# Clustered attention and two MLPs on one core: a pool per weight buffer, two products ahead of each second layer, the last MLP 1 pair by batch

## The chip, the core and the metric

The kernel runs on one core of a Trainium2 chip. The metric is the device time of one execution in microseconds (us). Five engines work beside each other: TensorE (PE in the profile; its weight loads stand as PEld), VectorE (DVE), ScalarE (ACT), GpSimd (POOL) and SyncE (SP), which issues the DMAs. Each takes its own instructions in order and waits on semaphores for the others.

## What is computed

Three blocks follow each other. Two batches, eight heads, 768 positions, head size 64; the two MLPs have 1536 tokens, a model width of 512, and inner widths of 2048 and 1536.

```python
mask = argmax(q_n . c_n) == argmax(k_n . c_n)           # same cluster of 16
attn = softmax(where(mask, scale * q @ k.T, -1e9)) @ v
x = attn, heads side by side                            # (1536, 512)
h = x @ w_in;   x = (h * sigmoid(h)) @ w_out            # MLP 1
out = (sigmoid(x @ w_gate) * (x @ w_val)) @ w_out2      # MLP 2
```

The weights come as 64-bit floats. All matmuls have operands split into a high and a low half, and three products (high x high, high x low, low x high) make one.

## The kernel before

**Order.** The kernel is written against a planner that places each engine's instructions: they have the priority of the order in which the code issues them, and the planner takes what it reckons to be ready. A tile pool gets a stretch of memory; pools that are closed give theirs to pools opened later, which then wait for the work on what lay there. Tiles of one tag in a pool share its buffers.

**Attention** (L101 to L529) runs over eight pairs of heads, four per batch. `raw` and `st` hold a pair's loaded and split queries and keys until `prep` (L328) has prepared it, `hd` (L105, one pool per parity of the pair) its heads and values, `cp` tables, among them `q2` and `k2` of both parities (L207), and `wk` what goes from step to step. `finish` (L457) scales a pair's result into `acc` (L54), which holds the activations between the blocks. For batch 0, the operands of MLP 1 are made on POOL during the second half of attention (L476 to L481).

**Operands.** `right_operands` (L73) makes seven operands per batch from the four blocks of `acc` in the manner of Strassen: 11, 21, t2, t1, t3, t4, 22, with four additions, seven casts to a high half (ACT) and seven subtractions for the low half (DVE or POOL). It yields eight times.

**MLP 1** takes the inner width in eight pairs of 128-column blocks (`N1`, L540). `hidden` (L686) computes a pair by `strassen` (L637): seven products x, y, x again, z, v, w, w again, each of twelve matmuls for both batches or six for one. `take` applies SiLU, and `split` (L677) writes the high half (ACT) and the low half (POOL or DVE) into the four buffers of `gp`. `mixed` (L700) is the second layer: it multiplies them into `acc`, in four or six tiles that `accumulate` (L694) adds, on DVE, or copies for pair 0, on ACT. Pair 0 runs batch by batch; so does the second layer of the last pair, and the operands of MLP 2 are made after each batch of it (`operands`, L727, y).

**MLP 2** has six pairs (`N2`). `gated` (L747) runs `strassen` twice, for the gate and for the value, `out_of` (L766) is its second layer, in six tiles of twelve matmuls.

**Weights.** A job (L601) makes one weight: `converted` (L542) loads 512 KB into one of two buffers `rp` and builds 32-bit words from it on ACT, POOL and DVE; `two` (L558) splits into high and low halves, in seven buffers of `sp`, used in turn. `seven` (L570), for a first layer, takes three of them and one of two small ones (tag d); `plain`, for a second layer, takes one; so an MLP 1 pair takes 5, an MLP 2 pair 8. `weights` (L621) starts the jobs up to two ahead of the one asked for.

**Banks.** `pp` (L538) has four buffers of two PSUM banks, for products and second layers alike. The buffer of x is held from the first to the second half of x, that of w likewise.

These are the lines that the change moves against each other (L790):

```python
    for i in range(N2):
        for bs in (slice(0, 1), slice(1, 2)) if i == 0 else (ALL,):
            gated(i, bs)
        out_of(i)
```

Of the kernel before, what the change touches and what calls it, by code (L numbers as in the profile page):

```python
# [10 lines left out]
F32 = mybir.dt.float32  # L11
# [20 lines left out]
def clustered_attention_then_two_mlps(ctx, tc, qT, kT, v, cen, w1i, w1o, w2g, w2v, w2o, out):  # L32
# [40 lines left out]
    def right_operands(pool, temporary, name, b, caster, adder, subbers):  # L73
# [25 lines left out]
        yield  # L99

    with ExitStack() as att:  # L101
        raw = att.enter_context(tc.tile_pool(name="raw", bufs=1))
        st = att.enter_context(tc.tile_pool(name="st", bufs=1))

        hd = {p % 2: att.enter_context(tc.tile_pool(name=f"hd{p}", bufs=1)) for p in (NPAIR, NPAIR + 1)}  # L105
        cp = att.enter_context(tc.tile_pool(name="cp", bufs=1))
        wk = att.enter_context(tc.tile_pool(name="wk", bufs=2))
        sm = att.enter_context(tc.tile_pool(name="sm", bufs=4))
# [67 lines left out]

        wt = cp.tile([P, 512], BF16, tag="wt", name="wt")
        nc.vector.memset(wt, 0.0)
# [27 lines left out]

        q2, k2 = ([cp.tile([P, 2, S], R32, tag=f"{nm}_{i}", name=f"{nm}_{i}") for i in range(2)] for nm in ("q2", "k2"))  # L207

# [119 lines left out]
        def prep(p):  # L328
# [56 lines left out]
            for i in range(NT):  # L385
                nc.tensor.transpose(pt[:, i * P : (i + 1) * P], o[:, i].rearrange("p j n c -> p (j n c)"), identb)
            rows = wk.tile([P, S], F32, tag="rb", name=f"rows{p}")
            nc.scalar.activation(rows, pt[:, 0:S], AF.Identity, bias=rowbias, scale=rowscale)
# [9 lines left out]
        def scores(p, j, i):  # L398
            qa, qm, ka, km, _ = heads[p]
            s = ps_s.tile([P, 2, 512], F32, tag="s", name=f"s{p}_{j}_{i}")  # L400
            for n, (a, c) in enumerate(((qa, ka), (qm, km))):
                for g in range(2):
                    nc.tensor.matmul(  # L403
                        s[:, g, 0:HS],
                        lhsT=a[:, j, i * P : (i + 1) * P],
                        rhs=c[:, j, g * HS : (g + 1) * HS],
                        start=n == 0,
                        stop=n == 1,
                    )
            nm = sm.tile([P, 1], F32, tag="nm", name=f"nm{p}_{j}_{i}")  # L410
            nc.vector.tensor_reduce(nm, s[:, :, 0:HS], axis=AX.XY, op=ALU.max, negate=True)  # L411
            e = wk.tile([P, 2, HS], F32, tag="e", name=f"e{p}_{j}_{i}", bufs=4)
            if p not in tots:
                tots[p] = wk.tile([P, 2 * NT], F32, tag="tot", name=f"tot{p}")
# [23 lines left out]
        def values(p, j, g):  # L438
# [14 lines left out]
            if p not in xf:  # L453
                xf[p] = wk.tile([P, S], F32, tag="xf", name=f"xf{p}")
            nc.vector.tensor_tensor(xf[p][main, g * G : (g + 1) * G], o[main], other[main], op=ALU.add)  # L455

        def finish(p):  # L457
# [3 lines left out]
            nc.vector.tensor_scalar_add(t, t, 1e-9)  # L461
            rs = wk.tile([P, 2 * NT], F32, tag="rs", name=f"rs{p}")
# [3 lines left out]
            rt = wk.tile([P, P], F32, tag="rt", name=f"rt{p}")  # L466
            nc.scalar.activation(rt[0 : 2 * NT], pr[0 : 2 * NT, 0:P], AF.Copy)
            yield
            rb = wk.tile([P, S], F32, tag="rb", name=f"rb{p}")
            dma_rows(rb, rt)  # L470
# [86 lines left out]

    def two(src, name, tag="w", bufs=None):  # L558

        n = src.shape[1]  # L560
# [9 lines left out]
    def seven(srcs, name):  # L570
# [12 lines left out]
        s34 = two(t[:, 2:4].rearrange("p a b -> p (a b)"), f"{name}t")  # L583
        last = two(a22, f"{name}d", tag="d", bufs=2)

# [51 lines left out]
    def strassen(w, name, take, bs):  # L637
# [19 lines left out]
        u2 = temporary(f"{name}u")[:, bs]  # L657
        nc.scalar.activation(u2, x, AF.Copy)
        add(u2, run(bank(f"{name}y"), "s2", "t2"), u2)
        run(xb, "a12", "21", start=False)  # L660
        take(x, 0, 0, bs, False)
        u3 = temporary(f"{name}v")[:, bs]
        add(u3, run(bank(f"{name}z"), "s3", "t3"), u2)
        c21 = temporary(f"{name}c")[:, bs]
        nc.vector.tensor_tensor(c21, u3, run(bank(f"{name}v"), "a22", "t4"), op=ALU.subtract)
        take(c21, 1, 0, bs, True)
        qb = bank(f"{name}w")
        q = run(qb, "s1", "t1")
        add(u3, q, u3)
        take(u3, 1, 1, bs, True)  # L670
        run(qb, "s4", "22", start=False)
        add(u2, q, u2)
        take(u2, 0, 1, bs, True)

    gs = {}
# [10 lines left out]
    def hidden(i, bs):  # L686
# [4 lines left out]

        strassen(weights("1i", i), f"h{i}", take, bs)

# [6 lines left out]
    def mixed(i, b=None):  # L700
# [9 lines left out]
        for n, c in enumerate(parts):  # L710
            for e in range(2):
# [3 lines left out]
                for d in range(2):  # L715
                    for k, (fh, fl) in enumerate(f):
                        for m, (s, t) in enumerate(((wh, fh), (wh, fl), (wl, fh))):
# [6 lines left out]
                            )  # L724
                accumulate(z[:, 2 * e : 2 * e + 2, c], o[:, :, 0:width], i == 0)

    def operands(pool, name, b):  # L727
        for _ in right_operands(pool, temporary, name, b, nc.scalar, nc.vector, [nc.vector, nc.gpsimd]):
            pass

    for i in range(N1):
        if i == 0:
            for b in range(B):
                if b:
                    operands(tp, "x", b)
                hidden(i, slice(b, b + 1))
                mixed(i, b)
            continue
        hidden(i, ALL)
        if i < N1 - 1:  # L740
            mixed(i)
            continue
        for b in range(B):
            mixed(i, b)
            operands((xp, tp)[b], "y", b)

    def gated(i, bs):  # L747
# [11 lines left out]

        strassen(weights("2g", i), f"g{i}", gate, bs)  # L760
        strassen(weights("2v", i), f"v{i}", value, bs)

# [3 lines left out]
    def out_of(i):  # L766
        f = [[gs[f"b{i}", k, t].rearrange("p h b s -> p (h b s)") for t in "hl"] for k in range(2)]
        for t in range(0, B * S // P, 2):
# [14 lines left out]
            if i == N2 - 1:  # L783
                for a in range(2):
# [61 lines left out]
```

## Time and profile before

| | us |
|---|---|
| median of 3 runs (lowest to highest) | 885.61 (883.98 to 886.31) |
| the profiled execution | 891.42 |
| its span, first to last instruction | 889.6 |
| PE busy in it | 810.3 (91%) |
| DVE busy | 656.0 (74%) |
| POOL busy | 462.4 (52%) |
| ACT busy | 396.1 (45%) |

All durations below are of the profiled execution. A timeline row has the start, the time, the engine, the line, the operation, the tile written and the tiles read, with the shape; brackets hold the idle time of that engine before it and who ended it. Tile names have lost their numbers: `ghb` and `glb` are the high and low halves of a pair's activations in MLP 2 (`gha`, `gla` in MLP 1), `z` a second-layer tile of MLP 2 (`y` in MLP 1), `wh` and `wl` halves of a weight; `x11h` to `xt4l` are operands of MLP 1, `y11h` to `yt4l` of MLP 2.

### The profile page before, as it was taken

How to read it: one execution, taken by the hardware profiler on the slowest of the kernel's cores; microseconds unless marked ns; L12 is line 12 of the kernel's file. 1: busy time of each engine (PE TensorE's matmuls, PEld its weight loads, DVE VectorE, ACT ScalarE, POOL GpSimd, SP SyncE). 2: the span in 40 equal slices, each digit the busy share in tenths (PEclk: the TensorE clock that was granted, in tenths of full speed). 3: DMA queues.
4: the chain of work that ended last, by engine and by line, in shares of the span. 5: the costliest groups of instructions: out<-in, count | busy, mean ns of one | idle time of the engine just before them, and what ended most of it. 6: DMA issues, size and time to landing. Idle time of an engine off the chain costs nothing.

```text
span 889.6 us, 12086 instructions
## 1 busy us (share of the span) xinstructions
PE 810.3 (91%) x4539; PEld 699.0 (79%) x4539; DVE 656.0 (74%) x822; ACT 396.1 (45%) x679; POOL 462.4 (52%) x390
## 2 busy tenths in 40 slices
PE   6899999999996788999999999399969989898997
PEld 4777777777774687988988898398958969697896
DVE  5778877987986877687677668957784776757635
ACT  3556556556666554424524434444521514234020
POOL 4512260582307776547546557758682745747221
PEclk9999999999999799999999999689998989799899
DMA  7564465356310222121121120002221211111003
GB/s 214 142 156 110 115 165 132 100 143 153 122 43 19 95 95 90 53 95 48 48 95 48 48 95 24 25 24 93 73 70 50 72 47 67 53 48 48 1 1 142
DMA packets 25226, 72.50 MB, mean 81 GB/s; under 512 B 4144, under 2 KB 4240, under 8 KB 25168
## 3 DMA queue, kind: packets, MB, share of 16 engines
q1 hardware_dynamic: 25168, 71.73, 27.1%
q8 instruction: 36, 0.59, 0.3%
q14 instruction: 22, 0.18, 0.1%
HBM read 48.27 MB, written 3.19 MB: 58 GB/s over the span
## 4 chain that ended last, share of the span: by engine, by line
PE 66%; DVE 22%; ACT 4%; issue 4%; POOL 3%; DMA 1%; SPq 0%; DVEq 0%; ACTq 0%; POOLq 0%
PE z L774 10%; PE s L403 7%; PE v L443 6%; PE t L435 4%; PE h_0x L643 3%; PE g_0w L643 3%; PE v_0x L643 3%; DVE nm L411 3%; PE pm L140 2%; PE v_0w L643 2%; PE g_0x L643 2%; DVE gla L684 2%; PE u L430 2%; PE y_10None L718 2%; PE y_21None L718 2%
## 5 line engine op out<-in xcount | busy, mean ns | idle before, releaser
L416 ACT ACTIVATE e<-s,nm 128x768 f32<-128x768 f32 x96 | 86.5, 902 | 67.4 <-DVE nm L411 66.4
L411 DVE TENSOR_REDUCE nm<-s 128x1 f32<-128x768 f32 x96 | 90.9, 950 | 10.8 <-PE s L403 8.3
L443 PE MATMUL v<-ph,vv 128*64 128x256 f32 x576 | 75.5, 389 | 1.4 <-DVE xf L455 1.2
L774 PE MATMUL z<-whu,ghb 128*128 128x512 f32 x144 | 61.2, 425 | 14.0 <-ACT ghb L59 10.2
L403 PE MATMUL s<-ka,qa 128*128 128x384 f32 x192 | 59.5, 391 | 6.5 <-ACT e L416 6.4
L774 PE MATMUL z<-whu,glb 128*128 128x512 f32 x144 | 58.4, 434 | 4.7 <-DVE glb L684 4.7
L774 PE MATMUL z<-wlu,ghb 128*128 128x512 f32 x144 | 60.6, 421 | 0.0
L435 PE MATMUL t<-ident,e 128*128 128x128 f32 x384 | 57.9, 280 | 1.2 <-DVE ph L62 1.0
L443 PEld LDWEIGHTS v<-ph,vv 128*64 128x64 f32 x576 | 37.4, 137 | 24.9 <-issue 6.7
L698 DVE TENSOR_TENSOR acc<-z,acc 128x1024 f32<-128x1024 f32 x30 | 36.6, 1223 | 24.2 <-PE z L774 24.1
L403 PE MATMUL s<-k,q 128*128 128x384 f32 x192 | 51.6, 350 | 1.0 <-DVE k L320 1.0
L435 PEld LDWEIGHTS t<-ident,e 128*128 128x128 f32 x384 | 45.2, 143 | 6.9 <-issue 1.9
L341 POOL TENSOR_SCALAR qq<-qq 128x768 f32<-128x768 f32 x7 | 5.8, 834 | 82.5 <-DMA qq<-in_qT 70.3
L774 PEld LDWEIGHTS z<-whu,ghb 128*128 128x128 f32 x144 | 29.7, 206 | 22.7 <-ACT ghb L59 12.3
L403 PEld LDWEIGHTS s<-ka,qa 128*128 128x128 f32 x192 | 29.9, 195 | 20.4 <-ACT e L416 11.7
L474 POOL TENSOR_TENSOR acc<-xf,rb 128x768 f32<-128x768 f32 x7 | 12.8, 1832 | 58.8 <-DMA rb<-d_rb 52.5
L774 PEld LDWEIGHTS z<-whu,glb 128*128 128x128 f32 x144 | 30.1, 209 | 15.8 <-DVE glb L684 9.5
L59 ACT ACTIVATE ph<-t 128x512 f32<-128x512 f32 x48 | 28.6, 596 | 21.1 <-PE t L435 20.8
L430 PE MATMUL u<-ident,e 128*128 128x128 f32 x192 | 36.8, 280 | 0.2 <-DVE ph L62 0.2
L455 DVE TENSOR_TENSOR xf<-v,other 64x256 f32<-64x256 f32 x48 | 20.1, 419 | 22.3 <-ACT other L452 22.0
L403 PEld LDWEIGHTS s<-k,q 128*128 128x128 f32 x192 | 35.4, 194 | 1.5 <-DVE k L320 1.5
L62 DVE COPY ph<-t 128x512 f32<-128x512 f32 x48 | 32.7, 680 | 4.7 <-PE t L435 4.6
(1441 smaller groups left out, 2561.0 us busy)
## 6 DMA issues: line engine op xcount, KB each, us to landing
ri<-in_w1i SPq DMA_DIRECT2D x16, 512.0 KB, 3.2
ro<-in_w1o SPq DMA_DIRECT2D x16, 512.0 KB, 3.2
ka<-kh SPq DMA_DIRECT2D x32, 192.0 KB, 3.7
rg<-in_w2g SPq DMA_DIRECT2D x12, 512.0 KB, 3.2
rv<-in_w2v SPq DMA_DIRECT2D x12, 512.0 KB, 3.3
ru<-in_w2o SPq DMA_DIRECT2D x12, 512.0 KB, 3.1
qq<-in_qT SPq DMA_DIRECT2D x8, 384.0 KB, 4.8
kk<-in_kT SPq DMA_DIRECT2D x8, 384.0 KB, 4.6
```

The lines of the kernel that those rows point to most:

```text
L59: return nc.scalar.activation(o, i, AF.Copy)
L62: return nc.vector.tensor_copy(o, i)
L403: nc.tensor.matmul(s[:, g, 0:HS], lhsT=a[:, j, i * P : (i + 1) * P], rhs=c[:, j, g * HS : (g + 1) * HS], start=n == 0, stop=n == 1,)
L411: nc.vector.tensor_reduce(nm, s[:, :, 0:HS], axis=AX.XY, op=ALU.max, negate=True)
L416: nc.scalar.activation(e, s[:, :, 0:HS], AF.Exp, bias=nm, scale=1.0, accum_out=tots[p][:, n : n + 1])
L430: nc.tensor.transpose(both[:, kt - 4, i % GT, :], e[:, kt * P : (kt + 1) * P], ident)
L435: nc.tensor.transpose(t[:, kt, :], e[:, kt * P : (kt + 1) * P], ident)
L443: nc.tensor.matmul(o[(L, U)[kt % 2]], lhsT=vv[:, j, kt, :], rhs=ph[:, kt, :], start=kt < 2, stop=kt >= NT - 2,)
L643: nc.tensor.matmul(o[:, b, 0:HS], lhsT=w[a][s][:, k, :], rhs=right[b, q][t][:, k, :], start=start and k == 0 and n == 0, stop=k == KQ - 1 ...
L698: nc.vector.tensor_tensor(z, o, z, op=ALU.add)
L718: nc.tensor.matmul(o[:, d, 0:width], lhsT=s[:, d, k, :], rhs=t[:, c], start=k == 0 and m == 0, stop=k == 1 and m == 2,)
L774: nc.tensor.matmul(o[:, a, :], lhsT=s[:, (t + a) * P : (t + a + 1) * P], rhs=r, start=k == 0 and n == 0, stop=k == 1 and n == 2,)
```

## The change

- `rp` is opened ahead of attention and shares no memory with it. `q2` and `k2` get pools of their own (`qk`), each beside the `hd` pool of its parity. The tiles that a pair's end needs (`tot`, `xf`, `rs`, `rt`, `rb`) move from `wk` to a pool `fin` at the end.
- `sp` becomes seven pools of one buffer, each with a high and a low half, used in turn: five behind `wp` and the small pair's `dp`, two behind `up` and `gp`.
- `strassen` and `mixed` yield after each product and each tile, so that the loop over stages (pair, or pair and batch) can lay two generators side by side.
- Of each stage but a few, the first two products are issued ahead of the second layer of the stage before (`FRONT`): not for batch 1 of MLP 1's pair 0, and not for batch 1 of MLP 2's pair 0, whose batch 0 has no second layer of its own.
- The operands of MLP 1 for batch 1 are issued beside the products of batch 0 instead of after its second layer.
- The last pair of MLP 1 runs batch by batch altogether; the operands of MLP 2 are issued beside its second layers and the products of the stage after.

```diff
+    rp = ctx.enter_context(tc.tile_pool(name="rp", bufs=2))
     with ExitStack() as att:
...
-        hd = {p % 2: att.enter_context(tc.tile_pool(name=f"hd{p}", bufs=1)) for p in (NPAIR, NPAIR + 1)}
+        hd, qk = {}, {}
+        for p in (NPAIR % 2, (NPAIR + 1) % 2):
+            hd[p] = att.enter_context(tc.tile_pool(name=f"hd{p}", bufs=1))
+            qk[p] = att.enter_context(tc.tile_pool(name=f"qk{p}", bufs=1))
+        wk = att.enter_context(tc.tile_pool(name="wk", bufs=2))
         cp = att.enter_context(tc.tile_pool(name="cp", bufs=1))
-        wk = att.enter_context(tc.tile_pool(name="wk", bufs=2))
+        fin = att.enter_context(tc.tile_pool(name="fin", bufs=2))
...
-    rp = ctx.enter_context(tc.tile_pool(name="rp", bufs=2))
     wp = ctx.enter_context(tc.tile_pool(name="wp", bufs=3))
-    sp = ctx.enter_context(tc.tile_pool(name="sp", bufs=7))
+    dp = ctx.enter_context(tc.tile_pool(name="dp", bufs=2))
+    NSP = 7
+    sp = [ctx.enter_context(tc.tile_pool(name=f"sp{n}", bufs=1)) for n in range(NSP - 2)]
     up = ctx.enter_context(tc.tile_pool(name="up", bufs=8))
     gp = ctx.enter_context(tc.tile_pool(name="gp", bufs=1))
+    sp += [ctx.enter_context(tc.tile_pool(name=f"sp{n}", bufs=1)) for n in range(NSP - 2, NSP)]
+    taken = iter(range(10000))
...
-        hi = sp.tile([P, n], R32, tag=f"{tag}h", name=f"{tag}h{name}", bufs=bufs)
-        lo = sp.tile([P, n], R32, tag=f"{tag}l", name=f"{tag}l{name}", bufs=bufs)
+        w = (pool or sp[next(taken) % NSP]).tile([P, 2, src.shape[1]], R32, tag="w", name=f"w{name}")
+        hi, lo = w[:, 0], w[:, 1]
...
+    stages = []
+    for i in range(N1):
+        for b in range(B) if i in (0, N1 - 1) else (None,):
+            stages.append(("1", i, b))
     for i in range(N2):
-        for bs in (slice(0, 1), slice(1, 2)) if i == 0 else (ALL,):
-            gated(i, bs)
-        out_of(i)
+        for b in range(B) if i == 0 else (None,):
+            stages.append(("2", i, b))
+
+    def front(kind, i, b):
+        return (hidden if kind == "1" else gated)(i, ALL if b is None else ONE[b])
+
+    beside = operands(tp, "x", 1)
+    gen = front(*stages[0])
+    for n, (kind, i, b) in enumerate(stages):
+        steps(gen, beside)
+        following = stages[n + 1] if n + 1 < len(stages) else None
+        if following is not None:
+            gen = front(*following)
+        late = kind == "1" and i == 0 and b == 0
+        if following is not None and not late and not (kind == "2" and b == 0):
+            steps(gen, n=FRONT)
+        if kind == "1":
+            if i < N1 - 1:
+                steps(mixed(i, b), beside)
+                run(beside)
+            else:
+                run(beside)
+                beside = operands((xp, tp)[b], "y", b)
+                parts = mixed(i, b)
+                for c in range(4):
+                    next(parts)
+                    if c in (1, 2):
+                        next(beside)
+                run(parts)
+        elif b != 0:
+            run(beside)
+            out_of(i)
```

`steps` runs one generator and lays a step of another behind each of its steps, `run` runs one to its end, `FRONT` is 2, and `ONE[b]` selects one batch.

## Rows read from the trace of the kernel before

**Rows 1.** Windows by stage: PE, PEld, DVE, ACT, POOL us; clock; DMA; GB/s.

```profile
270.50:359.00 88.50, 71.20 (x338) 63.01 (x338) 69.87 (x73) 48.46 (x79) 66.59 (x56) 0.90 0.22 76
359.00:521.00 162.00, 156.18 (x782) 139.97 (x781) 115.50 (x127) 65.62 (x96) 92.25 (x80) 1.00 0.19 65
521.00:621.70 100.70, 83.81 (x422) 78.56 (x421) 77.81 (x83) 45.65 (x71) 69.56 (x54) 0.90 0.13 44
621.70:884.60 262.90, 243.91 (x1200) 219.68 (x1199) 174.98 (x172) 81.18 (x119) 138.21 (x119) 0.94 0.16 55
```

**Rows 2.** Chain of waits: start, us, engine, tile, line, count; starts of pairs.

```profile
359.05 2.10 PE h_0x L643 x12
521.16 2.10 PE h_0x L643 x12
621.70 2.10 PE g_0x L643 x12
679.11 2.10 PE g_0x L643 x12
838.97 2.10 PE g_0x L643 x12
870.22 14.34 PE z L774 x63
```

**Rows 3.** PE at MLP 2's boundaries: chain row, timeline (in brackets: idle before).

```profile
761.58 2.12 PE v_0w L643 x12
...
665.88 0.79 PE L774 MATMUL z<-whu,ghb 128*128 128x512 f32 x1 [2.97 <-DVE acc L698]
...
767.79 0.79 PE L774 MATMUL z<-whu,ghb 128*128 128x512 f32 x1 [2.72 <-ACT ghb L59]
771.39 0.80 PE L774 MATMUL z<-whu,glb 128*128 128x512 f32 x1 [0.85 <-DVE glb L684]
```

**Rows 4.** Windows: the stretch behind one boundary, columns as in rows 1.

```profile
770.00:780.00 10.00, 9.15 (x27) 6.83 (x26) 7.85 (x8) 0.00 (x0) 3.22 (x3) 0.62 0.14 52
```

**Rows 5.** Timeline there: POOL's weight half, DVE's split and accumulation.

```profile
751.92 1.30 POOL L564 TENSOR_TENSOR wlg4s<-sg,whg4s 128x512 fp32r<-128x512 f32 x1 [4.53 <-ACT whg4s L59]
...
768.76 2.57 DVE L684 TENSOR_TENSOR glb<-g_0v,ghb 128x768 fp32r<-128x768 f32 x1
783.67 1.23 DVE L698 TENSOR_TENSOR acc<-z,acc 128x1024 f32<-128x1024 f32 x1 [0.77 <-PE z L774]
```

**Rows 6.** Timeline at a boundary of MLP 1: POOL, PE.

```profile
457.13 1.29 POOL L564 TENSOR_TENSOR wli6s<-si,whi6s 128x512 fp32r<-128x512 f32 x1
...
478.24 0.50 PE L718 MATMUL y_10None<-gla,who 128*128 128x512 f32 x1 [1.17 <-DVE gla L684]
```

**Rows 7.** Timeline of the passage out of attention: ACT, POOL, PE, DVE.

```profile
225.35 0.68 ACT L551 ACTIVATE ci<-ri 128x512 f32<-128x512 f32 x1
...
263.08 1.83 POOL L474 TENSOR_TENSOR acc<-xf,rb 128x768 f32<-128x768 f32 x1 [20.07 <-DMA rb<-d_rb]
...
270.95 0.63 ACT L59 ACTIVATE whi0a<-ci 128x512 fp32r<-128x512 f32 x1
...
284.51 0.44 PE L643 MATMUL h_0w<-x22h,whi0t 128*128 128x384 f32 x1 [3.26 <-DVE h_0v L669]
...
295.20 0.95 DVE L70 TENSOR_TENSOR xt4l<-xt,xt4h 128x768 fp32r<-128x768 f32 x1
...
295.65 0.69 PE L718 MATMUL y<-gha,who 128*128 128x384 f32 x1 [4.80 <-ACT who L59]
```

**Rows 8.** Timeline of the passage between the MLPs: POOL, DVE, PE.

```profile
561.20 2.51 POOL L70 TENSOR_TENSOR y21l<-acc,y21h 128x768 fp32r<-128x768 f32 x1
...
561.97 2.55 DVE L70 TENSOR_TENSOR yt2l<-yt,yt2h 128x768 fp32r<-128x768 f32 x1
...
564.58 0.69 PE L643 MATMUL g_0y<-yt2l,whg0s 128*128 128x384 f32 x1 [6.02 <-DVE yt2l L70]
...
577.49 0.95 DVE L70 TENSOR_TENSOR yt4l<-yt,yt4h 128x768 fp32r<-128x768 f32 x1
```

More of the change, by code (lines that the diff above doesn't have):

```diff
@@ L174, in clustered_attention_then_two_mlps @@
         dma(kk, kT[0, 0])
-        wt = cp.tile([P, 512], BF16, tag="wt", name="wt")
+        wt = fin.tile([P, S], F32, tag="rb", name="wt").bitcast(BF16)[:, 0:512]
         nc.vector.memset(wt, 0.0)
@@ L203, in clustered_attention_then_two_mlps @@
         nc.scalar.activation(identb, ident, AF.Copy)
-        q2, k2 = ([cp.tile([P, 2, S], R32, tag=f"{nm}_{i}", name=f"{nm}_{i}") for i in range(2)] for nm in ("q2", "k2"))
+        q2, k2 = ([qk[i].tile([P, 2, S], R32, tag=nm, name=f"{nm}_{i}") for i in range(2)] for nm in ("q2", "k2"))
         oh = [cp.tile([P, NT, 2, 2, 32], BF16, tag=f"oh_{i}", name=f"oh_{i}") for i in range(2)]
@@ L386, in prep @@
                 nc.tensor.transpose(pt[:, i * P : (i + 1) * P], o[:, i].rearrange("p j n c -> p (j n c)"), identb)
-            rows = wk.tile([P, S], F32, tag="rb", name=f"rows{p}")
+            rows = fin.tile([P, S], F32, tag="rb", name=f"rows{p}")
             nc.scalar.activation(rows, pt[:, 0:S], AF.Identity, bias=rowbias, scale=rowscale)
@@ L413, in scores @@
             if p not in tots:
-                tots[p] = wk.tile([P, 2 * NT], F32, tag="tot", name=f"tot{p}")
+                tots[p] = fin.tile([P, 2 * NT], F32, tag="tot", name=f"tot{p}")
             n = j * NT + i
@@ L453, in values @@
             if p not in xf:
-                xf[p] = wk.tile([P, S], F32, tag="xf", name=f"xf{p}")
+                xf[p] = fin.tile([P, S], F32, tag="xf", name=f"xf{p}")
             nc.vector.tensor_tensor(xf[p][main, g * G : (g + 1) * G], o[main], other[main], op=ALU.add)
@@ L461, in finish @@
             nc.vector.tensor_scalar_add(t, t, 1e-9)
-            rs = wk.tile([P, 2 * NT], F32, tag="rs", name=f"rs{p}")
+            rs = fin.tile([P, 2 * NT], F32, tag="rs", name=f"rs{p}")
             nc.vector.reciprocal(rs, t)
@@ L583, in seven @@
         s34 = two(t[:, 2:4].rearrange("p a b -> p (a b)"), f"{name}t")
-        last = two(a22, f"{name}d", tag="d", bufs=2)
+        last = two(a22, f"{name}d", dp)
         def part(pair, n):
@@ L666, in strassen @@
         take(c21, 1, 0, bs, True)
+        yield
         qb = bank(f"{name}w")
@@ L673, in strassen @@
         take(u2, 0, 1, bs, True)
+        yield
     gs = {}
@@ L690, in take @@
             split(g, m, h, bs, f"a{i}", nc.gpsimd if h == 0 else nc.vector)
-        strassen(weights("1i", i), f"h{i}", take, bs)
+        yield from strassen(weights("1i", i), f"h{i}", take, bs)
     def accumulate(z, o, first):
@@ L725, in mixed @@
                 accumulate(z[:, 2 * e : 2 * e + 2, c], o[:, :, 0:width], i == 0)
+                yield
     def operands(pool, name, b):
[L728 to L745, printed above, removed]
+        return right_operands(pool, temporary, name, b, nc.scalar, nc.vector, [nc.vector, nc.gpsimd])
     def gated(i, bs):
@@ L788, in out_of, with steps, run @@
                     nc.sync.dma_start(out[n : n + P, :], z[:, a])
-    for i in range(N2):
-        for bs in (slice(0, 1), slice(1, 2)) if i == 0 else (ALL,):
-            gated(i, bs)
-        out_of(i)
+    def steps(main, beside=iter(()), n=None):
+        for _ in main:
+            next(beside, None)
+            if n is not None:
+                n -= 1
+                if n == 0:
+                    return
+    def run(gen):
+        for _ in gen:
+            pass
+    ONE = [slice(b, b + 1) for b in range(B)]
+    FRONT = 2
+    stages = []
+    for i in range(N1):
+        for b in range(B) if i in (0, N1 - 1) else (None,):
+            stages.append(("1", i, b))
+    for i in range(N2):
+        for b in range(B) if i == 0 else (None,):
[28 more added lines that the diff above has]
+            out_of(i)
 def _layout(i):
```

16 lines of the change are left out of this document (10 added, 6 removed).

## Prediction

> **What bounds the kernel now.** I read the busy time by stage first [rows 1]. The two MLPs run from 270.5 to 884.6 us. TensorE (PE) is the fullest engine in each of their four stages: 71.2 of 88.5 us in the passage out of attention, 156.2 of 162.0 in the steady part of MLP 1, 83.8 of 100.7 in the passage between the MLPs, 243.9 of 262.9 in the rest of MLP 2. VectorE (DVE) comes next with 69.9, 115.5, 77.8 and 175.0. So the question is what PE needs and what it loses.
>
> The chain of waits gives the need [rows 2]. A product of twelve 384-column matmuls takes 2.10 us, so one batch's half takes 1.05. The last 63 matmuls of 512 columns take 14.34 us, 0.228 each, so the 72 of one pair's second layer take 16.4. An MLP 1 pair needs 7 x 2.10 + 16.4 = 31.1 us, an MLP 2 pair 14 x 2.10 + 16.4 = 45.8; the last pair of MLP 2, from 838.97 to 870.22 + 14.34, takes 45.6, so this price is reached where nothing stands in the way. By batch a second layer is 96 matmuls of 384 columns, 96 x 2.10/12 = 16.8.
>
> What is lost, by the starts in [rows 2]:
> - Passage 1, from the end of attention (about 271.0, [rows 7]) to 359.05: 88.1 us for pairs 0 (14.7 + 16.8) and 1 (31.1), 62.6. Lost 25.5.
> - MLP 1, 359.05 to 521.16: five pairs at 32.4 against 31.1. Lost 1.3 each, 6.6 in all.
> - Passage 2, 521.16 to 621.70: 100.5 us for the last pair of MLP 1 (14.7 + 16.8) and pair 0 of MLP 2 (29.4 + 16.4), 77.3. Lost 23.2.
> - MLP 2: 621.70 to 679.11 is 57.4, the three pairs up to 838.97 take 53.3 each, against 45.8. Lost 11.6 + 3 x 7.5 = 34.1.
>
> Together 89 us. The profiled execution is 891.4 us, 889.6 of it span; the median of the three timed runs is 885.6, so 5.8 come off at the end.
>
> **Products ahead of the second layer, MLP 2.** PE's rows at one boundary [rows 3]: pair 3's last product ends at 763.70, some second-layer matmuls follow, then PE waits 2.72 us for ScalarE (ACT) and 0.85 for DVE, 3.6 in all. The other 4 us of the 7.5 are clock: in 770 to 780, after the wait, the granted clock is 0.62 of 2.4 GHz, so three quarters of that stretch ran at the 1.2 GHz level [rows 4]. The change puts two products of the next pair, 4.2 us, where the wait is. They must be ready then: the low half of the second weight they need is done at 753.2, ten us early [rows 5]. So 4.2 covers 3.6, and with PE kept busy I take the clock's fall to go too. MLP 1 supports that: its boundary wait of 1.17 us [rows 6] leaves the stage's clock at 1.00 [rows 1].
>
> What is late next is a bank. Four double banks serve products and second layer. The put-ahead product x holds one until its second half runs behind the second layer, y one until DVE has added it, so the second layer has two or three. One wait of this sort is there already: 2.97 us for the accumulation on DVE [rows 3]. An accumulation takes 1.23 us against 12 x 0.228 = 2.7 of PE work per bank [rows 5], which two banks bear unless DVE is held up; a split beside GpSimd (POOL) takes 2.57 [rows 5]. So I leave 2 to 2.5 us at each of four boundaries and take 25 of 34.1. Bounds: everything, 34; or the waits alone while the clock still falls, 4 x 3.6 = 14.
>
> The Trainium skill (Perfetto Trace Analysis, Matmul Optimizations and Identifying Performance Opportunities) wants all eight PSUM banks in use and reads a gap that repeats as a possible lack of buffers; it speaks against holding a bank. The 2.97 us above agree with it once; what it would do at every tile is rival 4.
>
> **The same in MLP 1.** The wait is 1.17 us [rows 6]; the next pair's first weights are done at 458.4, 20 us before that wait [rows 6]. 4.2 us cover it. I take 5.5 of 6.6 (bounds 2 and 6.6).
>
> **A pool per weight buffer, passage 1.** Added up from the tiles in the code, the seven weight buffers were one stretch from 18 to 50 KiB behind `acc` and its neighbours, over the heads of both pair parities. The trace shows that a pool waits for all it lies over: weight words were converted into `wp`, which lies over dead memory, at 225.35, but the first high half `whi0a` starts at 270.95 [rows 7], when the last pair's values are read. Now `sp0` lies where `st` was and `sp1` to `sp4` over pair 6's heads and tables; with `dp` they are the five buffers that pair 0 needs (3 + 1 + 1). Pair 6 is finished by 263.08 [rows 7], so its memory is free before that, and POOL stood idle for the 20.07 us before that row.
>
> So these leave the passage: four 1.3 us subtractions of 512 columns on POOL (price as in [rows 5]), the small one, one more conversion, and the casts on ACT. PE's waits behind them were 4.80 us on `who`, plus part of 3.26 at batch 0's last product, where DVE had been busy with words and operands [rows 7]. The operands of batch 1 then have DVE and POOL nearly to themselves: they ended at 296.15 [rows 7]. I take 6 us off, an estimate: near 8 us of POOL's work leaves, part of which lay beside DVE's. That is 290, while PE has 7.4 + 8.4 = 15.8 us of batch 0 from 271.6, to 287 to 289. Pair 1's first two products stand ahead of batch 1's second layer as in the steady part. I leave 8.5 us: 17 gained. Bounds: 6 (the 4.80 and the start of the lows), 22 (all but the start, and 2 for the first operands).
>
> In attention the moved work costs something: some 8 us POOL, 4 ACT, 2 DVE, under PE's work. POOL is idle there. The loads of the jobs that start earlier go out on SP behind the last pair's loads; behind them on SP stand only the small DMAs of `finish`, for which batch 1's operands wait but no product of batch 0. I take 2 us; bounds 0 (all hidden) and 4 (all of ACT's on the path).
>
> **MLP 1's last pair by batch, passage 2.** PE waited here for operands of MLP 2: 6.02 us for one low half [rows 8], and the stage's clock is 0.90 [rows 1]. DVE and POOL work in each other's way: a 768-element subtraction on DVE takes 2.55 with POOL's beside it and 0.95 alone [rows 8].
>
> The Trainium skill (SBUF — State Buffer, Who interferes with whom) has DVE instructions with two SBUF inputs and POOL's block each other for a whole instruction. The 2.55 against 0.95 agree. By it one batch's operands are one queue of 7 DVE and 4 POOL instructions, whatever the order.
>
> By the rows a batch takes 7 x 0.95 to 7 x 2.55, about 14 us with POOL's. Before, batch 0's operands had 8.4 us of PE work over them (batch 1's second layer), batch 1's nothing that could run. Now batch 0's have 5.3 (five products) + 8.4 = 13.7, and batch 1's have the first pair's 14 half products, 14.7. That covers them nearly; left are the DVE work of the products themselves and the order. Pair 1's products ahead of the first second layer of MLP 2 come on top. DVE's 77.8 us [rows 1] are a floor for the stage unless its collisions shrink. I leave 9: 14.5 gained. Bounds: 5.3 (only the five products) and 20.
>
> Splitting the pair costs PE nothing: 14 half products are 14.7 as before, and its second layer was by batch already. The new pool order in attention (`qk`, `fin`) changes no instruction: nothing, unless memory collides, which the same number of buffers excludes.
>
> **The sum.** 25 + 5.5 + 17 - 2 + 14.5 = 60. 891.4 - 60 = 831.4 for a profiled execution; 885.6 - 60 = 825.6, called 825. The low bounds give 14 + 2 + 6 - 4 + 5.3 = 23, or 862; the high ones 34 + 6.6 + 22 + 20 = 83, or 803.
>
> **Rivals.**
> 1. Everything is covered, PE runs at its price but for the ends: 803 to 808. For it: nothing but PE is near full. Against it: DVE has 69.9 of 88.5 and 77.8 of 100.7 in the passages.
> 2. The other engines keep a wait at each boundary, and the clock falls with it: passages 12 + 8, MLP 1 3, MLP 2 16, cost 3: 36, or 850. For it: splits that take 2.57 at the boundary, one queue with the new product's addition. Against it: x and y need nothing from those splits.
> 3. The change doesn't do what it says: the planner orders by when it believes things ready, and may put the next pair's products behind the second layer as before, so that only the passages gain, 12 + 12: 862. Against it: the weights are ready ten us and more ahead.
> 4. Slower, by banks. With x held, the second layer runs on two banks, and a tile waits whenever its accumulation stands behind other DVE work. There are 78 such tiles (48 in MLP 1, 30 in MLP 2). 2.97 at each, the wait of [rows 3], would be 232; it decides against the 60 gained from 0.77 us a tile. At 1.2 a tile it would be 94 - 60 = 34 slower, 920. For it: that one row. Against it: one in 36 tiles of MLP 2 before, and two banks bear 1.23 against 2.7.
>
> **How the numbers follow.** Forecast (810 to 840) 0.62, rival 1 0.09, rival 2 0.19, rival 3 0.05, rival 4 0.05. The range 806 to 852 leaves out half of rival 1, a third of rival 2 (840 to the low bounds' 862), and 3 and 4: 0.2. A measurement of this kernel tells 0.3%, 2.7 us, from no change: faster 0.93, within it 0.02 (between rivals 3 and 4), slower 0.05.
>
> **What would show it.** The chain's starts: pairs of MLP 1 every 31 to 31.5 us, of MLP 2 every 47 to 48.5; no stretch of MLP 2's steady part at a granted clock near 0.6; in PE's timeline x and y of the next pair between the last product and the second layer. `whi0a` before 265, no wait on `who`. MLP 2's operands of batch 0 under products of batch 1. Wrong would be: second-layer matmuls that wait for accumulations at most boundaries (rival 4), MLP 2 pairs still above 51 (rival 2), or attention ending more than 4 us later.

## The result, and the profile after

The changed kernel takes 843.82 us (median; 843.03 to 848.22) against 885.96 (883.98 to 887.90) for the kernel before in the same session: a ratio of 0.9535, 95% interval 0.9495 to 0.9574. That is 42 us less; the forecast was 60 less. The profiled execution took 843.03 us, 841.2 of it span, against 891.4: 48.4 less, because the profile of before lay 5.5 above its median and that of after 0.8 below.

The same windows as [rows 1], cut at the stages of the changed kernel: the two passages, each with the steady part behind it (span of the window and its length, then busy time of each engine with its instructions, granted clock, DMA share, GB/s).

```profile
core 0: us, PE busy (x) PEld busy (x) DVE busy (x) ACT busy (x) POOL busy (x), PEclk, DMA share, GB/s
276.30:357.30 81.00, 69.44 (x355) 64.81 (x356) 57.74 (x59) 43.28 (x67) 47.65 (x39) 0.92 0.18 57
357.30:512.80 155.50, 155.50 (x778) 140.28 (x777) 124.58 (x128) 64.69 (x95) 90.10 (x80) 1.00 0.20 69
512.80:609.90 97.10, 82.82 (x426) 77.87 (x425) 81.00 (x92) 49.66 (x83) 73.79 (x58) 0.95 0.14 48
609.90:842.00 232.10, 226.30 (x1183) 210.19 (x1181) 168.99 (x169) 81.07 (x117) 133.12 (x118) 1.00 0.18 64
```

Both steady parts are full: PE is busy for all 155.5 us of MLP 1, and in MLP 2 for 226.3 of 232.1, the rest being the end of the output. The granted clock is 1.00 in both (0.94 in MLP 2 before). In the passages PE is still idle for 12 and 14 us.

The chain of waits of the same kernel gives the pairs: start, us, engine, tile, line, count. A pair's `z` starts where the second layer of the pair before it ends, as its `x` and `y` are done by then.

```profile
361.52 2.10 PE h_0z L650 x12
...
485.95 2.10 PE h_0z L650 x12
...
614.08 2.10 PE g_0z L650 x12
...
659.88 2.10 PE g_0z L650 x12
...
705.47 2.10 PE g_0z L650 x12
...
796.87 2.10 PE g_0z L650 x12
...
821.88 14.34 PE z L772 x63
```

Four pairs of MLP 1 take 124.4 us, 31.1 each; those of MLP 2 45.7 (182.8 us for four). Both are the price in [rows 2]: before, 32.4 and 53.3.

The edit puts two products ahead, but the planner lays a third among the first tiles of the second layer: the second half of `x`, which reads `y21h` and `y21l`. PE's timeline at one boundary of MLP 2:

```profile
634.74 0.51 PE L650 MATMUL g_0x<-y11h,wg2a 128*128 128x384 f32 x2
...
641.69 0.52 PE L650 MATMUL g_0x<-y21h,wg2a 128*128 128x384 f32 x2
...
645.07 0.51 PE L650 MATMUL g_0x<-y21h,wg2a 128*128 128x384 f32 x2
```

So 6.3 us of the next pair (three products of 2.1) are done before its `z`, and the starts 359.05, 521.16 and 621.70 of [rows 2] correspond to 355.2, 510.7 and 607.8 here, each 2.1 earlier than the edges of the windows above (355.2 is 361.5 - 6.3, 510.7 is 485.95 + 31.1 - 6.3, 607.8 is 614.1 - 6.3). Stage by stage, the 48.3 us by which the last second layer ends earlier, at 836.2 instead of 884.5:

| stage | predicted | measured | from |
|---|---|---|---|
| attention | -2 | -5.8 | last values matmul ends at 276.26, before 270.5 |
| passage 1 | +17 | +9.6 | 88.5 to 78.9 |
| MLP 1, five pairs | +5.5 | +6.6 | 162.1 to 155.5 |
| passage 2 | +14.5 | +3.4 | 100.5 to 97.1 |
| MLP 2, five pairs | +25 | +34.4 | 262.8 to 228.4 |
| sum | +60 | +48.2 | |

Attention, timeline of PE and ACT (brackets: idle time before, and who ended it). First the kernel before, a values matmul that both kernels reach at the same time:

```profile
234.62 1.52 PE L443 MATMUL v<-ph,vv 128*64 128x256 f32 x12
```

The changed kernel:

```profile
234.59 1.52 PE L448 MATMUL v<-ph,vv 128*64 128x256 f32 x12
...
266.26 0.66 ACT L559 ACTIVATE co<-ro 128x512 f32<-128x512 f32 x1 [3.44 <-DMA ro<-in_w1o]
...
267.86 0.44 PE L435 MATMUL u<-ident,e 128*128 128x128 f32 x2 [1.91 <-ACT e L421]
270.06 0.69 PE L435 MATMUL u<-ident,e 128*128 128x128 f32 x2 [1.07 <-ACT e L421]
...
274.74 1.52 PE L448 MATMUL v<-ph,vv 128*64 128x256 f32 x12 [0.73 <-DVE xf L460]
```

From there to the last values matmul it is 40.15 us; before, the last one starts at 268.99, so 34.4. At 262.8 ACT's queue stood for 3.44 us on a weight load of pair 1, with the exponentials behind it, and PE waited for those.

Passage 1, what answers [rows 7]: PE, then DVE ahead of the second of PE's two waits.

```profile
286.98 0.69 PE L732 MATMUL y<-gha,wo 128*128 128x384 f32 x1 [2.80 <-ACT gha L59]
292.91 0.69 PE L732 MATMUL y<-gha,wo 128*128 128x384 f32 x1 [5.25 <-DVE h_0v L673]
...
284.00 2.03 DVE L561 TENSOR_SCALAR ci<-ci 128x512 int32<-128x512 int32 x1
285.95 2.56 DVE L82 TENSOR_TENSOR xt<-acc 128x768 f32<-128x768 f32 x1
288.43 1.48 DVE L562 SCALAR_TENSOR_TENSOR ci<-ri,ci 128x512 int32<-128x512 int32 x1
289.84 2.55 DVE L84 TENSOR_TENSOR xt<-acc,xt 128x768 f32<-128x768 f32 x1
292.31 0.54 DVE L673 TENSOR_TENSOR h_0v<-h_0z,h_0u 128x384 f32<-128x384 f32 x1
```

The wait on `who` is gone, and the last product, which waited 3.26 us, now runs at 301.2, behind the first half of this second layer, without a wait. New is one on `h_0v`, an addition of 0.54 us for a product that PE had done by 281. Ahead of it DVE has 8.6 us of weight words and of batch 1's operands. What PE waits for is a bank: the four buffers are used in turn, and by that order the second tile of the second layer takes the one that this addition reads.

Passage 2, what answers [rows 8]: PE's waits, then ACT and DVE in the middle of them.

```profile
545.09 0.62 PE L732 MATMUL y<-gha,wo 128*128 128x384 f32 x2 [3.33 <-ACT gha L59]
548.07 0.69 PE L732 MATMUL y<-gla,wo 128*128 128x384 f32 x1 [2.35 <-DVE gla L698]
563.49 0.45 PE L650 MATMUL v_0y<-yt2h,wv0s 128*128 128x384 f32 x1 [2.13 <-DVE g_0v L673]
569.79 0.48 PE L650 MATMUL g_0w<-y22h,wg0t 128*128 128x384 f32 x1 [3.94 <-DVE g_0v L681]
...
538.96 1.28 ACT L750 ACT_TABLE_LOAD   x1
540.76 1.28 ACT L703 ACT_TABLE_LOAD   x1
...
537.56 2.13 DVE L70 TENSOR_TENSOR yt2l<-yt,yt2h 128x768 fp32r<-128x768 f32 x1
539.62 2.04 DVE L70 TENSOR_TENSOR yt4l<-yt,yt4h 128x768 fp32r<-128x768 f32 x1
541.58 0.54 DVE L685 TENSOR_TENSOR h_1u<-h_1w,h_1u 128x384 f32<-128x384 f32 x1
```

The wait for an operand (6.02 in [rows 8]) is down to 0.93 and 0.54. In its place the last second layer of MLP 1 waits for its own activations: `h_1u` stands on DVE behind 4.2 us of low halves of MLP 2's operands, and then 1.9 us on ACT (542.1 to 544.0) behind other steps. The two waits behind, 2.13 and 3.94 us, are for banks again: `g_0v` at L681 reads the bank in which the second half of `w` goes on, and the one at L673, by the order of the buffers, the bank that `v_0y` takes. ACT loads a table for one Sigmoid and another back to Silu.

### The profile page after: what moved, and what is told of

Its sections match the earlier page's. It is cut to its first block, busy times and chain, and to the rows that moved or that the text cites. A ratio compares the mean times of both kernels' runs of the same rounds, so it can differ in the third digit from the quotient of the medians.

```text
span 841.2 us, 12031 instructions
## 1 busy us (share of the span) xinstructions
PE 790.9 (94%) x4539; PEld 691.0 (82%) x4539; DVE 658.0 (78%) x829; ACT 399.4 (47%) x690; POOL 456.1 (54%) x392
## 4 chain that ended last, share of the span: by engine, by line
PE 80%; DVE 13%; ACT 3%; issue 2%; DMA 1%; POOL 0%; SPq 0%; ACTq 0%; DVEq 0%; POOLq 0%
PE z L772 12%; PE s L408 6%; PE v L448 6%; PE y L732 4%; PE h_0w L650 3%; PE t L440 3%; PE h_0x L650 3%; DVE nm L416 3%; PE v_0w L650 3%; PE g_0w L650 3%; PE v_0x L650 3%; PE pm L145 3%; PE g_0x L650 2%; PE y_00None L732 2%; PE y_10None L732 2%; PE y_01None L732 2%
## 5 line engine op out<-in xcount | busy, mean ns | idle before, releaser
L772 PE MATMUL z<-wu,ghb 128*128 128x512 f32 x288 | 88.2, 390 | 0.0
L772 PEld LDWEIGHTS z<-wu,ghb 128*128 128x128 f32 x288 | 53.8, 188 | 10.0
L772 PE MATMUL z<-wu,glb 128*128 128x512 f32 x144 | 54.3, 392 | 0.0
L732 PE MATMUL y<-gha,wo 128*128 128x384 f32 x128 | 38.9, 373 | 13.3 <-ACT gha L59 8.1
L346 POOL TENSOR_SCALAR qq<-qq 128x768 f32<-128x768 f32 x7 | 5.8, 831 | 82.7 <-DMA qq<-in_qT 66.4
L732 PEld LDWEIGHTS y<-gha,wo 128*128 128x128 f32 x128 | 26.3, 213 | 15.4 <-ACT gha L59 9.6
```

What stands on the lines that cost most here:

```text
L732: nc.tensor.matmul(o[:, d, 0:width], lhsT=s[:, d, k, :], rhs=t[:, c], start=k == 0 and m == 0, stop=k == 1 and m == 2,)
L772: nc.tensor.matmul(o[:, a, :], lhsT=s[:, (t + a) * P : (t + a + 1) * P], rhs=r, start=k == 0 and n == 0, stop=k == 1 and n == 2,)
```

## The experiments

Executions differ by some us before 235 us already (the first of the two values matmuls starts between 233.9 and 240.4), so two stretches are compared, not clock times: passage 1, from the end of the last values matmul to the end of pair 1's second layer (85.2 us in the changed kernel), and passage 2, from the end of pair 5's second layer to that of MLP 2's first pair (128.2). Both hold the products put ahead at their ends. Attention's end is taken as the time between the two values matmuls above (34.4 before, 40.1 after).

### What brings the 42 us

```diff
-        if following is not None and not late and not (kind == "2" and b == 0):
+        if False:
```

> The changed kernel with no product issued ahead of a second layer; everything else as changed. Theory A (the two products ahead of the second layer close the steady boundaries, and nothing else does): MLP 1 pairs go back from 31 to 32.4 us and MLP 2 pairs from 45.6 to about 53 with the clock falling at each boundary, so 36 + 7 us are lost: 880 to 892. Theory B (the steady parts run faster because each weight buffer is now released by itself): MLP 2 pairs stay below 48, total below 856.

Measured: 882.67 us (881.06 to 886.14), ratio to before 0.9957 (0.9940 to 0.9973). PE's waits in its MLP 2 (total, times, longest):

```profile
PE z L772 <- ACT ghb L59: 9.8, 4, 2.5
PE z L772 <- DVE glb L698: 5.7, 7, 1.5
PE v_0w L650 <- DVE v_0v L681: 2.8, 4, 1.6
```

Without the products ahead MLP 2 takes 262.1 us, as before (262.8). The pairs of MLP 1 take 31.7 us. The other parts of the change together are worth 3.6 us against the kernel before in the same session (886.26).

```diff
-    FRONT = 2
+    FRONT = 1
```

> The changed kernel with one product ahead (x alone) instead of two. Theory A with the cover as the point (3.6 us of wait need 4.2 us of work): 2.1 us leave 1.5 us of wait at each MLP 2 boundary; if a wait that short no longer lets the clock fall, a pair takes 47 to 47.5, in all 848 to 852; if the clock falls as before, 50 to 51 and 860 to 866. Theory C (the order at the boundary matters, not the length of the cover): 842 to 846.

Measured: 847.05 us (844.10 to 849.02), ratio 0.9545 (0.9509 to 0.9582). Its MLP 2: two of PE's waits, and windows right behind them.

```profile
642.19 0.50 PE L772 MATMUL z<-wu,glb 128*128 128x512 f32 x1 [2.32 <-DVE glb L698]
...
691.41 0.50 PE L772 MATMUL z<-wu,glb 128*128 128x512 f32 x1 [1.60 <-DVE glb L698]
...
642.00:646.00 4.00, 3.81 (x10) 3.04 (x11) 2.80 (x3) 0.63 (x1) 2.71 (x3) 0.59 0.05 10
692.00:696.00 4.00, 4.00 (x19) 3.33 (x18) 3.93 (x5) 0.63 (x1) 1.99 (x3) 1.00 0.11 20
```

One product leaves 2.32 us of wait at the first boundary, where the clock falls, and 1.6 at each of the other three, where it stays and a pair takes 47.6 us. With two the waits are gone. The planner moves the second half of `x` up in both kernels, so PE has 4.2 us of the next pair here and 6.3 with two. Passage 2, however, is 120.8 us here, 7.4 shorter than with two: this led to the kernels with one ahead in passage 2 alone, below.

### Passage 1 and attention

```diff
-    sp = [ctx.enter_context(tc.tile_pool(name=f"sp{n}", bufs=1)) for n in range(NSP - 2)]
     up = ctx.enter_context(tc.tile_pool(name="up", bufs=8))
     gp = ctx.enter_context(tc.tile_pool(name="gp", bufs=1))
-    sp += [ctx.enter_context(tc.tile_pool(name=f"sp{n}", bufs=1)) for n in range(NSP - 2, NSP)]
+    sp = [ctx.enter_context(tc.tile_pool(name=f"sp{n}", bufs=1)) for n in range(NSP)]
```

> The changed kernel with all seven weight buffers laid behind the other pools, over memory of the last pair, so that no high or low half can be made before attention ends. Theory A (early weights cost attention nearly what they save behind it): attention ends 3 to 6 us earlier (last values at 270 to 273 instead of 276), PE waits for weights in the first passage as before the change, total 840 to 849. Theory D (early weights are worth the 17 us forecast, and attention ends later for another reason): attention still ends at 276, total 855 to 861.

Measured: 841.92 us (840.08 to 842.71), ratio 0.9490 (0.9465 to 0.9516): no slower than the changed kernel. PE in its attention:

```profile
236.44 1.52 PE L448 MATMUL v<-ph,vv 128*64 128x256 f32 x12
...
271.51 1.52 PE L448 MATMUL v<-ph,vv 128*64 128x256 f32 x12 [0.73 <-DVE xf L460]
```

Attention's end takes 35.1 us again, 5 less; passage 1 takes 88.5, 3.3 more. The changed kernel and the four others whose edits lie behind passage 1 have 85.3 to 88.4 there, so the 3.3 are hardly above the scatter, but from the first of the two values matmuls to the end of pair 1 all five take longer (125.7 to 129.5) than this one (125.1). The eight kernels with the early buffers have 38.8 to 41.7 at attention's end (without the next one), the four with late ones 35.1 to 35.2. The early buffers move work of passage 1 under attention and lengthen attention by at least what the passage gains.

```diff
-        nc.scalar.activation(t, up_.bitcast(F32), AF.Copy, scale=2.0**-112)
+        with tc.issue_after(totalled[0].ins) if 3 <= len(made) else nullcontext():
+            nc.scalar.activation(t, up_.bitcast(F32), AF.Copy, scale=2.0**-112)
```

(`totalled` is the last `rt` activation of `finish`.)

> The weight words of pair 1 (jobs 3 and up) are converted on ACT only behind the last reciprocal rows of attention; pair 0's stay as early as they were. Theory A (attention ended 5.75 us later because ACT, at its front of the queue, waited 3.44 us for pair 1's words and then converted them among the last softmax rows): attention's last values end at 270.5 to 272.5 instead of 276.26, acc of the last pair is scaled by 277 instead of 281.26, time 838 to 841. Theory B (the end moved for another reason: DVE's and POOL's share, or the early words of pair 0): last values stay past 274.5, time 842 to 845.

Measured: 847.01 us (845.37 to 848.05), ratio 0.9551 (0.9509 to 0.9593). Attention's end takes 37.4 us: about half of the 5.8 came from pair 1's conversions in ACT's queue. That the rest comes from pair 0's early words is left over, not shown. Passage 1 becomes 90.6, as pair 1's words now lie in it. Theory A had the cause half and the time wrong.

```diff
-        steps(gen, beside)
+        steps(gen, beside if n else iter(()))
```

> Batch 1's x operands are traced behind batch 0's products of pair 0, not beside them; on DVE this moves the additions h_0v (L673), h_0c and the second h_0v ahead of the xt subtractions. Theory A (PE's longest wait in passage 1, 5.25 us at 292.91 for h_0v, is DVE's queue: the addition stood behind 8.6 us of operands and weight words): the wait on h_0v falls below 1.5 us, the second layer of batch 0 starts 3 to 5 us earlier, the operands of batch 1 end at most 2 us later, time 839 to 842. Theory B (the operands of batch 1 are the chain that counts, whatever stands ahead): the wait moves to pair 0's batch 1 products or pair 1's first product, time 843 to 846.

Measured: 844.39 us (842.43 to 846.71), ratio 0.9524 (0.9481 to 0.9568). Its PE in passage 1:

```profile
296.59 0.69 PE L650 MATMUL h_0w<-x22h,wi0t 128*128 128x384 f32 x1 [3.46 <-DVE h_0v L681]
```

The wait for the first `h_0v` is gone, as theory A had it; 3.46 us for the second one came in its place. Passage 1 is 82.7, 2.5 shorter, and the time is unchanged within its interval: closer to theory B.

### Passage 2

The last pair of MLP 1 for both batches, as before the change, and nothing put ahead of its second layer:

```diff
-        for b in range(B) if i in (0, N1 - 1) else (None,):
+        for b in range(B) if i == 0 else (None,):
...
-        if following is not None and not late and not (kind == "2" and b == 0):
+        if following is not None and not late and not (kind == "2" and b == 0) and following != ("2", 0, 0):
...
-                beside = operands((xp, tp)[b], "y", b)
-                parts = mixed(i, b)
...
+                for c in range(B):
+                    run(mixed(i, c))
+                    run(operands((xp, tp)[c], "y", c))
```

> The changed kernel with the last pair of MLP 1 for both batches at once, its second layer by batch and the operands of MLP 2 after each, as before the change; no products of MLP 2 ahead of that layer. Theory A (going by batch brought little, since the products' additions stand behind the operands on DVE): 844 to 850. Theory E (going by batch brought the 14.5 us forecast and something else lost them): 855 to 860. If going by batch cost something, below 842.

Measured: 847.87 us (846.34 to 850.38), ratio 0.9563 (0.9534 to 0.9592); passage 2 is 130.4. By batch, as it stands in the change, is worth 2 us in the profile and 4 between the medians. Against the next kernel, which goes by batch and likewise puts nothing ahead of the last second layer, it is 5.6 and 5.5.

```diff
-        if following is not None and not late and not (kind == "2" and b == 0):
+        if following is not None and not late and not (kind == "2" and b == 0) and following != ("2", 0, 0):
```

> The two gate products of MLP 2's pair 0, batch 0, are not put ahead of MLP 1's last second layer; everything else stays. Theory A (putting a Sigmoid product among Silu work costs more than it covers: two of the three table loads of 1.28 us in 538 to 565 exist for it): only one table load is left in the passage, PE's waits there on gha and gla (3.33 and 2.35) fall below 2 together, time 840 to 843. Theory B (the two half products cover what they cost): the waits on gha and gla grow by the 2.1 us of the products that are gone, time 845 to 848.

Measured: 842.41 us (841.04 to 844.57), ratio 0.9508 (0.9458 to 0.9559); passage 2 is 124.8. One table load is left in it, yet the waits on `gha` and `gla` did not fall (2.9 and 3.9 us). The edit also takes away the 2.1 us of products that ran before them, so what the loads alone cost isn't shown. The time agrees with theory A, its reason doesn't.

One product ahead before the gate alone, then also between the two batches of MLP 1's last pair:

```diff
-            steps(gen, n=FRONT)
+            steps(gen, n=1 if following == ("2", 0, 0) else FRONT)
```

> Two products ahead everywhere but before MLP 2's first pair, where one gate product (x) alone is put ahead of MLP 1's last second layer; so no Sigmoid falls among the Silu work and no second gate product asks for yt2 of batch 0 before that second layer. With one ahead everywhere (e2) the stretch from the end of MLP 1's pair 5 to the end of MLP 2's pair 0 was 120.8 us, against 128.2 with two and 124.8 with none at this one place. Theory A (that one product is what counts: x hides part of the wait, y brings the table loads and the wait on yt2): 120.5 to 122.5 us for that stretch, MLP 2 pairs at 45.6, time 836.5 to 839. Theory B (the 7.4 us come from the boundary between the two batches of MLP 1's last pair, or from the next boundary): 125 us or more, time 841 to 844.

```diff
-            steps(gen, n=FRONT)
+            steps(gen, n=1 if kind == "1" and i == N1 - 1 else FRONT)
```

> As e8, and one product ahead also between the two batches of MLP 1's last pair. Theory A (only the gate boundary counts): the same as e8 within 1 us, in the stretch and in the time. Theory B (the boundary between the batches counts as well): the stretch is 2 us or more shorter than in e8, 120 to 121 us, and the time 836 to 838.

Measured: 844.28 us (842.30 to 848.60), ratio 0.9525 (0.9479 to 0.9571), and 838.35 (835.53 to 840.05), 0.9458 (0.9412 to 0.9503). Passage 2 takes 126.4 and 120.7 us. PE's two long waits, in the kernel with one before the gate alone:

```profile
545.75 0.69 PE L732 MATMUL y<-gha,wo 128*128 128x384 f32 x1 [4.12 <-ACT gha L59]
550.30 0.69 PE L732 MATMUL y<-gla,wo 128*128 128x384 f32 x1 [3.86 <-DVE gla L698]
```

and what stands at that second layer in the other:

```profile
535.75 0.45 PE L732 MATMUL y<-gla,wo 128*128 128x384 f32 x1 [1.77 <-POOL gla L698]
...
544.48 0.44 PE L732 MATMUL y<-gla,wo 128*128 128x384 f32 x1 [0.16 <-DVE gla L698]
```

Four kernels with passage 2 as in the change have 126.5 to 128.2 us there, so the first kernel is at the edge of their scatter and the second 6 us below it. So theory B of both holds: the boundary between the batches is the place. There PE waits for nothing at the second layer. With two products put ahead the planner moves `h_1z` up into that second layer too; with one it does not. My reading was that what runs early is used up before the operands of MLP 2 come, and is missing when DVE and POOL work on them; the kernel with none between the batches, below, speaks against it in this form.

A wait for a bank is left in the better kernel too, behind an accumulation on DVE:

```profile
553.90 0.44 PE L650 MATMUL g_0v<-yt4h,wg0d 128*128 128x384 f32 x1 [3.21 <-DVE acc L712]
```

### Put together, and two tests on it

All seven weight buffers late, batch 1's operands behind the products, one product ahead in passage 2 (the edits above):

> As e9, with all seven weight buffers over the last pair's memory (as e3) and batch 1's x operands behind batch 0's products (as e5). If the three effects add: attention ends 3 us earlier, passage 1 shorter by up to 2.5, passage 2 by 7: 832 to 836. If passage 1 is bound by DVE's and POOL's words and operands however they are ordered, the earlier end of attention and the other order bring nothing together: pair 1's second layer ends at 360 to 362 as before, time 836 to 839, as e9.

Measured: 833.97 us (832.16 to 835.67), ratio 0.9402 (0.9362 to 0.9441). Attention's end is 35.2, passage 1 85.9, passage 2 121.1: the short attention of the late buffers, and passage 1 no longer than in the change. Against the kernel with one ahead in passage 2 alone it is 4 us, and those intervals touch. It beats the changed kernel by 10 us, and the intervals are apart.

```diff
-        if following is not None and not late and not (kind == "2" and b == 0):
+        if following is not None and not late and not (kind == "2" and b == 0) and following != ("1", N1 - 1, 1):
```

> As e10, with no product put ahead between the two batches of MLP 1's last pair. Theory A (in a passage a product put ahead where PE does not wait is taken from the work that should cover the next operands): the stretch from the end of pair 5 to the end of MLP 2's pair 0 falls from 121.1 us to 118.5 to 120.5, time 831.5 to 833.5. Theory B (one is as good as none: what e9 mended was the place of the y product on DVE's queue): 121 to 123 us, time 834 to 836.

Measured: 840.19 us (838.23 to 845.52), ratio 0.9475 (0.9432 to 0.9517); passage 2 takes 129.1. Both theories fall: none between the batches is worse than one, by 8 us in the profile and 6 between the medians. The planner still moves `h_1x` up, into the middle of the second layer of batch 0 (523.2). Its DVE, and PE behind it:

```profile
534.39 2.03 DVE L70 TENSOR_TENSOR yt2l<-yt,yt2h 128x768 fp32r<-128x768 f32 x1
536.34 0.54 DVE L675 TENSOR_TENSOR h_1c<-h_1v 128x384 f32<-128x384 f32 x1
...
536.94 0.44 PE L731 MATMUL y<-gha,wo 128*128 128x384 f32 x1 [2.28 <-DVE h_1c L675]
```

A subtraction of the product, which empties a bank, stands behind a 2.03 us low half once more. "The fewer ahead, the more cover" is too simple; what counts is how the products' additions fall among the operands on DVE. An order of DVE alone, with PE's kept, was not run, so this stays a reading of the traces.

The last kernel leaves out DVE's bit operations on the weight words of pair 1, so that these weights lack their low bits and sign:

```diff
+        if len(made) not in (3, 4, 5):
-        nc.vector.tensor_scalar(ti, ti, 3, None, op0=ALU.logical_shift_left)
+            nc.vector.tensor_scalar(ti, ti, 3, None, op0=ALU.logical_shift_left)
...
```

> As e10, with the three bit operations of DVE on the weight words of pair 1 (jobs 3 to 5, eight to nine instructions of 0.4 to 2.3 us in passage 1) left out, so that those weights lack their low bits and sign. Theory A (passage 1 is bound by DVE's queue, words and operands in line): from the last values matmul of attention to the end of pair 1 81.5 to 83.5 us instead of 85.9, time 831 to 833. Theory B (the operands and the low halves alone, DVE and POOL stretching each other, bind it; the words only fill gaps): 85 us or more, time 833.5 to 835.5.

Measured: 834.37 us (832.06 to 835.46), ratio 0.9397 (0.9360 to 0.9434); passage 1 is 85.1. Theory B: pair 1's words on DVE fill gaps and cost nothing that shows. Passage 1 of the kernel above without the 6.3 us put ahead at its end is 79.6, 17 above PE's price (62.6). That these belong to the operands, the splits and the low halves on DVE and POOL is argued, not shown: pair 0's words, the conversions on ACT and POOL and the lower clock are in them too.

## Why the prediction was off

The direction was right, the time lies within the range, and the likeliest value was 19 us too low: 825 against 843.8. By its steps:

- **MLP 2, right in mechanism, too small in size** (25, measured 34.4: all of the 34.1 that was lost, the upper bound). The table of PE's waits is empty from 610 to 842 us, so no bank is waited for there: the 2 to 2.5 us that I left at each boundary for banks don't exist, and pair 1 is down from 57.4 to 45.8 us. But the order was not the one I reckoned with. I had the second half of `x` behind the second layer; it ran among its first tiles, so the bank of `x` was not held over the whole layer, and what that would cost no run shows. Nor does the count "4.2 covers 3.6" hold as it stands: with 4.2 us of the next pair (one product ahead and its second half) 1.6 us of wait were left, and it took 6.3. That the planner moved a third product up was luck: nothing in the forecast counted on it. The Trainium skill (Perfetto Trace Analysis, Identifying Performance Opportunities) reads a repeating gap as a possible lack of buffers; the gap that repeated here, 2.7 us at MLP 2's boundaries, went with no buffer added. The clock went to 1.00 with the wait, as said.
- **MLP 1, right** (5.5, measured 6.6).
- **The early buffers, wrong** (15 net, with attention's cost). `whi0a`'s successor `wi0a` did start early, at 233.6, and the wait on `who` is gone: the mechanism is there. What failed is the price of the moved work. I took it to lie under PE's work in attention because POOL idled there; but it stands in ACT's queue among the exponentials, and in front of it stood a load. Bound 4, measured 5.8. The gain beside it, at most 3.3 us of passage 1 against the late layout, is a fifth of the 17 (the rest of the 9.6 is there with late buffers too): I priced POOL's work that leaves, and not that the operands of batch 1, on DVE and POOL, come after attention's end in any layout. I had named this as the sign of being wrong, attention over 4 us later, and it is what happened.
- **Passage 2, wrong in size** (14.5, measured 3.4; below its bound of 5.3). By batch works, 5.6 us between the two kernels with nothing ahead of the last second layer, and batch 0's operands lie under PE's work. I counted cover as time on PE and left the order on DVE at "9 us". The two products ahead, which I booked as coming on top, cost 7.4 us here: 10.8 are gained with one ahead everywhere (128.2 to 120.8), against 3.4 with two.
- **Banks, at the wrong place.** "What is late next is a bank" was said of MLP 2's boundaries, and none is late there. In the passages, where I put nothing down for it, PE waits 5.25, 2.13 and 3.94 us for banks that an addition on DVE has yet to read (the first two by the order of the buffers): rival 4's mechanism, though not at its places.
- **The sum.** The errors partly cancel: MLP 2 and MLP 1 came out 10.5 us better than forecast, attention and the passages 22 worse. That the time lies within the range owes something to this luck. Of the 19 us, 12 are these; the rest is mostly that I took gains read from an execution 5.8 us above its median off that median in full.
- **Rivals.** 843.8 lies near rival 2 (850), yet its mechanism is not what happened: PE keeps no wait at MLP 2's boundaries and no clock falls there. Rival 3, a planner that makes another order, spoils something at one place only, between the batches of the last pair.

## What to carry over

Put the next tile's independent products where PE waits: over the whole kernel they brought 39 of 42 us. Where PE doesn't wait, their number has to be tried, as they shift the order on the other engines: at such a boundary two cost 6 us against one, and none cost 6 to 8. Read in the trace what the planner made of the order before counting the cover. Work moved under an engine that idles is free only if none of the queues that it passes carries the critical chain: look at each of its instructions, ACT's and SP's too, and at what stands behind the first one that may wait for a load. Two edits that each stay within the noise alone (841.9 and 844.4 against 843.8) can add up to something worth having; try them together.

## What the runs showed of the hardware

- In the kernel with one product ahead, a wait of 1.60 us left the granted clock at 1.00, the 2.4 GHz level, in the 4 us behind it; a wait of 2.32 us with one of 0.75 shortly before it brought 0.59, mostly the 1.2 GHz level. So a shorter wait can give back more than itself: from none to one product ahead PE's listed waits in MLP 2 fell by 10.4 us (18.3 to 7.9), the time of MLP 2 by 22.9 (262.1 to 239.2).
- A table load on ACT took 1.28 us each time. The Trainium skill (ScalarE: Activation LUTs, What ACT_TABLE_LOAD costs) gives ~1283 ns for the load itself, which agrees, and 2.66 us for a switch with the drain that it adds, which does not: the ACT instruction before the load of 540.76 ends at 540.75, the one behind it starts at 542.06, 1.31 us later. Its section on table sets asks to finish one set before the next. With two loads fewer in passage 2 the waits on `gha` and `gla` behind them came to 6.9 us with no gate product ahead and 8.0 with one, against 5.7 with three loads and two products; what that rule would bring by itself no run here shows.
